# A linear-attention and token-mixing kernel: V kept in a two-tokens-per-partition layout

## The chip, the cores and the metric

One core of one Trainium2 chip. A core has TensorE (PE in the profile; its weight loads are shown apart as PEld), VectorE (DVE), ScalarE (ACT), GpSimd (POOL) and SyncE (SP, whose queue SPq issues the transfers that 16 DMA engines carry out). The metric is the device time of one execution in microseconds (us). Of several executions the median is given.

## The reference

```python
# r, k, v, w: (4 batches, 8 heads, 768 tokens, 48); u: (8, 48)
for t in range(S):
    cur = np.einsum('bhd,bhe->bhde', u[None] * kt, vt)
    y[:, :, t] = np.einsum('bhd,bhde->bhe', rt, state + cur)
    state = wt[:, :, :, None] * state + np.einsum('bhd,bhe->bhde', kt, vt)
...
x = attn_out.transpose(0, 2, 1, 3).reshape(B, S, H * D)      # (4, 768, 384)
wq, wk = x @ w_q, x @ w_k                                     # (4, 768, 64)
W_tok = scale * np.einsum('bsd,btd->bst', wq, wk)
out = np.maximum(np.einsum('bst,btd->bsd', W_tok, x), 0.0) @ w_out
```

Each head carries a 48 by 48 state that decays per key channel (w); each token adds the outer product of its key and value, and the current token counts with the extra weight u (the "bonus"). The second half mixes the tokens of a batch with a low-rank product and applies a linear layer. Since W_tok is a product of two 64-wide matrices, the kernel first forms wk^T x (64 by 384) for the batch and then multiplies by wq.

## The kernel before, in words

The recurrence is cut into chunks of 128 tokens. Two chunks make a unit of 256 tokens; 3 units make a batch, 12 units the whole. For a unit the kernel does, in the names of the steps (also the names of the tiles):

- **loads** (L489): w, k, r of 384 KB each, `load` at L237, with two consecutive tokens on a partition (64 partitions hold one chunk, so c = 0 and c = 1 are the two halves of the partitions, and j = 0, 1 is the token's parity). V comes in one of two ways, by the string `DIRECT` (L374): in 5 units like the others, in 7 units by four quarter loads (`load_v`, L229), which put one token on a partition, even tokens of a chunk on partitions 0 to 63, odd ones on 64 to 127.
- **ln, c16**: logarithm of w (lw), casts of k and r to 16 bits. **cw**: running sums of lw as matmuls with a mask. **ex**: en and ep, the exponentials of minus and plus the sum. **rT**: transposes of k and r on PE (kT, rT). **ks**: copy of kT. **qT** = rT x ks, **RT** = rT x ep, **KT** = ks x en, **ptm**: the chunk's total decay.
- **V**: in the 5 units a cast v16 (POOL, L601), four selection matmuls vp with PM (L605) that move V to one token per partition, and a copy VB out of PSUM (L615). In the 7 units only a cast VB (POOL, L596).
- **dps, dd, Vd**: the bonus weights of each token (matmuls of qT with u, L620), their copy (L630), and Vd = VB x dd on POOL (L635).
- **A, AM**: scores of a chunk, KT by RT, 16 matmuls a unit (48 rows in, 128 wide out, L643), masked by US on DVE (L653). US holds the causal mask times the key scale gv of a token.
- **kb, KD**: transposes of KT (L663) and their copy, scaled by gv (L673). **sn, SB**: the state before a chunk (a matmul of the identity with the old state, 384 columns) plus KD by VB (L684), and its decay on DVE (L698). The last chunk of a batch needs no new state.
- **y, X**: per chunk 8 matmuls of AM by VB, 48 columns each, and 4 of RT by the old state (L707); then X = y x gx + Vd on DVE (L738).
- **xt, xts, qk, qks**: transposes of X, their copy, the two projections and their copy. At the end of a batch **T** (wk^T X), then per unit **mx**, **rl** (ReLU), **fp** (by w_out), **os** and the **store**.

All matmuls go through `mm` at L191, so that the profile gives them one line and tells them apart by tile names: `PS<-VB,AM` is y's first part, `PS<-SB,RT` its second, `PS<-RT,KT` A, `PS<-CM,lw` cw, `PS<-v,PM` vp, `PS<-VB,KD` and `PS<-SB,ID` sn, `PS<-UB,qT` dps, `PS<-Z` fillers on zeros. Those that use 48 or 64 of the 128 rows of the array (cw, A, vp) come in twos on opposite halves.

The order of the work is a list made by a planner that runs while the program is built (class `Plan`). Every step has an engine, a duration, a rank and what it must follow; the planner starts the ready step of the lowest rank on each free engine, gives out the eight PSUM banks and the buffer rings, and the resulting order is the program's. Ranks are a long table of numbers (`RANK`, L312); `ENG` (L309) says for each unit which engine does a step that several could do (A for ACT, D for DVE, P for POOL). A PE step has a mode, 1 for those on half the rows; a step of the present mode has a bonus in rank (`stick`, here 10), and a change of mode is charged 90 ns. Fillers have the highest rank. Each engine then works its own list strictly in order.

Of the kernel before, what the change touches and what calls it, by code (L numbers as in the profile page):

```python
# [12 lines left out]
F32 = mybir.dt.float32  # L13
BF16 = mybir.dt.bfloat16
# [145 lines left out]
def kernel(  # L160
# [14 lines left out]
    C = 128  # L175
# [53 lines left out]
    def load_v(b, i, tl):  # L229

        for c in range(2):
            src = v[b, :, ds(i * U + c * C, C)].rearrange("h (q j) d -> j q h d", j=2)
            for j in range(2):
                nc.sync.dma_start(out=view(tl, c * DM, [[D, H], [1, D]], p0=64 * j, pn=64),  # L234
                                  in_=src[j])

# [7 lines left out]
    US = const([C, C], F32, "US")  # L244
# [4 lines left out]
    pos1 = const([C, 1], mybir.dt.int32, "pos1")  # L249
    gx = const([C, 1], F32, "gx")  # L250
    gv = const([C, 1], F32, "gv")
# [26 lines left out]
    for j in range(2):  # L278
        nc.gpsimd.iota(pos0[ds(64 * j, 64), :], pattern=[[0, 1]], base=j, channel_multiplier=2)
        nc.gpsimd.iota(pos1[ds(64 * j, 64), :], pattern=[[0, 1]], base=j + 1,  # L280
                       channel_multiplier=2)
# [14 lines left out]
    for j in range(2):  # L296
        m = view(US, 0, [[64, 2], [1, 64]], p0=j * 64, pn=64)
        nc.gpsimd.affine_select(m, m, pattern=[[1, 2], [2, 64]], compare_op=ALU.is_gt,
                                fill=0.0, base=-j, channel_multiplier=-2)

    nc.vector.tensor_scalar_mul(US, US, gv)

# [3 lines left out]
               KT=-956, ptm=-433, v16=-873, vp=-305, vb=-304, dps=-1398, vd=-510, A=-1752,  # L306
               am=2180, kb=370, kd=2179, sn=-276, sb=-57, y=-127, x=-406, xt=-2208, xts=-634,
               qk=796, qks=-45, T=-761, mx=134, rl=-215, fp=-10, os=-8, st=95, stick=-14)
    ENG = dict(k16="DPPPPPPPPPPP", r16="APPPPPPPPPPP", KT="DDPDPPPPPPPP", vb="AADDAAADAAAD",  # L309
               kd="AADAAAAAAAAA", xts="AAAAAAAADAAD", qks="AAAADAAAAAAA", rl="AAAAADAAAAAA",  # L310
               os="DAAAAAADADDA", dd="ADAAAAADAAAA", ks="DDDDDADDDADA")
# [3 lines left out]
            1000000, 1000000, 0, 17480, -4992, 450, 2230, -4819, 2230, 3580, -2227, 3580, 4930,  # L315
            315, 4930, 6280, 4423, 5750, 7042, 4130, 7599, 8203, 9637, 10305, 6520, 8450, 7220,
            9799, 9383, 8182, 7533, 10469, 8967, 9571, 10498, 9578, 10869, 10665, 11646, 12810,
            14571, 10180, 10943, 11020, 12143, 9340, 9491, 9540, 10180, 12085, 13085, 12245,
            14925, 17766, 13945, 15422, 16117, 16554, 20230, 20990, 3800, 7630, 8980, 5359, 6280,
            7630, 8120, 10330, 11680, 9560, 8980, 10330, 11886, 11510, 14832, 13007, 16113, 15138,  # L320
            12480, 15765, 15235, 18506, 17284, 16509, 15662, 15882, 15923, 17645, 17786, 18786,
            21226, 18161, 19234, 18493, 20634, 18127, 18462, 19791, 22267, 21533, 22901, 24034,
            22390, 19546, 24026, 24913, 25699, 27211, 12800, 15530, 16880, 6680, 11680, 13030,
            13880, 16880, 18230, 16380, 18230, 20230, 19932, 13171, 22133, 20817, 22948, 23977,
            14350, 23096, 11927, 25256, 24574, 22963, 25919, 25089, 26559, 27669, 28440, 25389,
            26460, 26289, 26366, 25169, 25926, 27682, 28802, 29266, 29636, 30172, 31267, 32025,
            33377, 34331, 35027, 36277, 42634, 44896, 45643, 47438, 68060, 64630, 65870, 40424,
            41218, 49147, 50444, 62246, 73160, 74400, 47931, 49305, 51271, 53304, 79580, 71920,
            73160, 18980, 20230, 21580, 21340, 22930, 24280, 22780, 24280, 25630, 25660, 26980,
            28980, 25521, 27610, 29917, 26889, 31321, 29263, 28642, 30827, 29432, 31862, 32532,  # L330
            31180, 30747, 31930, 32957, 33896, 32717, 34091, 37156, 33967, 36102, 34277, 34902,
            32317, 33017, 36557, 37244, 37511, 38427, 40144, 38057, 39136, 40754, 42035, 43054,
            43897, 19501, 21580, 22930, 24220, 25630, 26980, 27511, 28980, 30330, 32660, 34380,
            36380, 26366, 30967, 33370, 28102, 30292, 31980, 31877, 34497, 33214, 38466, 37784,
            34200, 32760, 39770, 39225, 39864, 42726, 42115, 43152, 38955, 41412, 36977, 40104,
            41298, 42554, 46608, 43554, 44151, 47308, 47764, 49883, 50497, 52931, 53981, 28540,
            30330, 31680, 29980, 31680, 33030, 31420, 33030, 34380, 37820, 40430, 42430, 34829,
            36326, 38633, 36017, 38171, 39200, 37617, 39984, 38875, 40684, 44834, 40556, 45863,
            45083, 42713, 42812, 49032, 48261, 49457, 49661, 50557, 43884, 46241, 47148, 48728,
            55306, 55676, 57228, 58272, 61887, 61643, 63369, 63826, 65200, 70240, 71791, 72987,  # L340
            74266, 78076, 76400, 77640, 68392, 70157, 75229, 75793, 77840, 79640, 80880, 78179,
            84333, 80138, 81398, 82371, 80880, 82120, 36040, 37730, 39080, 35460, 36380, 37730,
            40420, 42430, 43780, 42780, 46480, 48480, 43052, 44113, 49686, 44531, 47187, 48284,
            44758, 50831, 45385, 51474, 51799, 47560, 51346, 51566, 52629, 53486, 55438, 56273,
            59234, 57940, 58688, 53721, 54529, 50391, 52062, 55146, 57246, 60390, 61148, 62190,
            60765, 60925, 62492, 63450, 69605, 69158, 41000, 39080, 40430, 45229, 43780, 45130,
            48540, 49830, 51180, 52860, 55230, 57230, 47959, 50854, 54800, 54118, 52504, 57531,
            52116, 56126, 53151, 58894, 61199, 54277, 62137, 60557, 58699, 61966, 67582, 64953,
            61975, 62318, 63228, 60573, 62055, 63584, 64812, 66884, 65843, 66822, 67580, 68218,
            69299, 69630, 72169, 75340, 45660, 48480, 49830, 47100, 45130, 46480, 49980, 51180,  # L350
            52530, 61804, 58580, 60580, 54699, 58607, 62520, 57544, 59689, 60766, 47515, 51456,
            50715, 59283, 64030, 60716, 70782, 67826, 61497, 65731, 71002, 69344, 70247, 66715,
            67357, 63835, 64684, 70304, 71441, 71512, 72511, 73281, 76901, 77758, 78628, 80393,
            84435, 82119, 87246, 88696, 89206, 90963, 91363, 90071, 91311, 90536, 91283, 92601,
            93861, 94889, 93267, 94507, 92106, 92696, 94016, 95276, 95870, 94551, 95791, 51420,
            52530, 53880, 56567, 53880, 55230, 58347, 61930, 63280, 63845, 68570, 70570, 61097,
            63659, 66501, 65433, 69505, 69511, 66014, 70412, 67495, 71929, 72599, 68656, 73309,
# [592 lines left out]
```

## Time and profile before

| what | value |
|---|---|
| median of 3 runs | 107.58 us (107.21 to 109.12) |
| the profiled execution | 107.58 us, span of the instructions 105.9 us, granted clock 1.000 |
| units of PE work | 12, with 1503 matmul records |
| moved by DMA | 24.61 MB in 61,216 packets |
| transfers of V | 28 quarter loads of 96 KB, 5 whole ones of 384 KB |
| X on DVE (whole units) | 11 x 1014 ns |
| AM on DVE | 24 x 1219 ns |
| Vd on POOL (whole units) | 10 x 1480 ns |
| V casts on POOL | 12 x about 826 ns |

A busy share is the union of an engine's instructions over the span. Matmuls are pipelined: a record lasts from its start until its result is out, so records overlap and their mean length (183 ns for 48 columns) is far above the distance of two starts. Where the cost of a matmul matters, the starts in the timeline are read and not the lengths. A row of the timeline gathers neighbouring records of one form: start in us, length, engine, line, form, count.

### The profile page before, as it was taken

How to read it: one execution, taken by the hardware profiler on the slowest of the kernel's cores; microseconds unless marked ns; L12 is line 12 of the kernel's file. 1: busy time of each engine (PE TensorE's matmuls, PEld its weight loads, DVE VectorE, ACT ScalarE, POOL GpSimd, SP SyncE). 2: the span in 40 equal slices, each digit the busy share in tenths (PEclk: the TensorE clock that was granted, in tenths of full speed). 3: DMA queues.
4: the chain of work that ended last, by engine and by line, in shares of the span. 5: the costliest groups of instructions: out<-in, count | busy, mean ns of one | idle time of the engine just before them, and what ended most of it. 6: DMA issues, size and time to landing. Idle time of an engine off the chain costs nothing.

```text
span 105.9 us, 3705 instructions
## 1 busy us (share of the span) xinstructions
PE 97.4 (92%) x1503; PEld 69.9 (66%) x1506; DVE 86.8 (82%) x135; ACT 80.5 (76%) x121; POOL 72.4 (68%) x95
## 2 busy tenths in 40 slices
PE   5999899995988999899999799998977999999995
PEld 2346577574776698775879677895655777875651
DVE  6847789989979999979989999997686999863650
ACT  4338845986798699897999998995993798875630
POOL 6614399489796899999968998996089998000000
DMA  1999999899999989999996997899968950034374
GB/s 34 296 319 325 325 330 304 152 247 315 238 325 274 225 200 249 256 302 265 309 303 125 317 277 153 237 282 297 243 125 157 395 193 1 6 149 180 121 286 160
DMA packets 61216, 24.61 MB, mean 232 GB/s; under 512 B 58896, under 2 KB 60048, under 8 KB 61200
## 3 DMA queue, kind: packets, MB, share of 16 engines
q1 hardware_dynamic: 60640, 24.19, 84.6%
q10 hardware_dynamic: 560, 0.20, 0.7%
q8 instruction: 11, 0.18, 0.7%
q14 instruction: 5, 0.04, 0.1%
HBM read 19.66 MB, written 4.72 MB: 230 GB/s over the span
## 4 chain that ended last, share of the span: by engine, by line
PE 56%; DVE 10%; SPq 9%; POOL 9%; DMA 5%; ACT 4%; issue 3%; POOLq 0%; DVEq 0%; ACTq 0%
PE PS L191 56%; SPq L234 7%; POOL KT L582 6%; DVE AM L654 6%; DMA vg<-in_v_dram 5%; SPq L238 2%; ACT en L533 2%; POOL Vd L636 1%; DVE qT L564 1%; DVE X L741 1%; DVE SB L700 1%; ACT ep L539 1%; ACT ks L406 1%; ACT lw L502 1%; POOL r L510 1%
## 5 line engine op out<-in xcount | busy, mean ns | idle before, releaser
L654 DVE TENSOR_TENSOR AM<-PS,US 128x1024 bf16<-128x1024 f32 x24 | 28.7, 1219 | 2.7 <-PE PS L191 2.5
L636 POOL TENSOR_TENSOR Vd<-VB,dd 128x768 bf16<-128x768 bf16 (+1 forms) x14 | 18.1, 1294 | 4.0 <-ACT dd L406 2.1
L582 POOL TENSOR_TENSOR KT<-ks,en 128x1024 bf16<-128x1024 bf16 (+1 forms) x10 | 19.3, 1935 | 1.6 <-DVE ks L410 1.0
L191 PE MATMUL PS<-Z 128*128 128x512 bf16 x48 | 15.2, 443 | 1.3 <-DVE uT L256 1.2
L191 PEld LDWEIGHTS <-KT 48*128 48x128 bf16 (+1 forms) x272 | 10.5, 95 | 6.6 <-issue 3.9
L539 ACT ACTIVATE ep<-PS 128x1024 bf16<-128x1024 f32 (+1 forms) x14 | 12.8, 924 | 1.8 <-PE PS L191 1.8
L533 ACT ACTIVATE en<-PS 128x1024 bf16<-128x1024 f32 (+1 forms) x14 | 12.4, 901 | 2.2 <-PE PS L191 1.9
L741 DVE SCALAR_TENSOR_TENSOR X<-PS,gx,Vd 128x768 bf16<-128x768 f32 (+1 forms) x13 | 12.4, 953 | 2.0 <-PE PS L191 1.8
L191 PE MATMUL PS<-wo,MX 128*128 128x384 bf16 x72 | 13.3, 326 | 0.1
L502 ACT ACTIVATE lw<-wg 128x768 bf16<-128x768 f32 x12 | 10.1, 851 | 3.8 <-DMA wg<-in_w_dram 3.7
L408 ACT ACTIVATE KD<-PS,gv 128x1024 bf16<-128x1024 bf16 (+1 forms) x12 | 11.3, 945 | 1.9 <-PE PS L191 1.9
L510 POOL CAST k<-kg 128x768 bf16<-128x768 f32 x11 | 9.1, 826 | 4.3 <-PE PS L191 3.4
L700 DVE TENSOR_TENSOR SB<-PS,ptm 128x384 bf16<-128x384 f32 x20 | 11.0, 550 | 1.2 <-PE PS L191 1.2
L406 ACT COPY XT<-PS 128x768 bf16<-128x768 bf16 (+1 forms) x11 | 8.5, 773 | 2.9 <-PE PS L191 2.8
L406 ACT COPY os<-PS 128x768 f32<-128x768 f32 (+1 forms) x10 | 7.0, 703 | 3.9 <-PE PS L191 2.9
L510 POOL CAST r<-rg 128x768 bf16<-128x768 f32 x11 | 9.1, 824 | 1.1 <-DMA rg<-in_r_dram 1.1
L191 PEld LDWEIGHTS <-Z 128*128 128x128 bf16 x51 | 5.0, 109 | 6.7 <-issue 2.8
L191 PE MATMUL PS<-VB,AM 128*128 128x48 bf16 x192 | 8.4, 183 | 0.9 <-DVE AM L654 0.8
L191 PEld LDWEIGHTS <-MX 128*128 128x128 bf16 x72 | 6.5, 98 | 3.9 <-issue 0.2
L191 PE MATMUL PS<-RT,KT 48*128 48x128 bf16 x192 | 9.0, 218 | 0.0
L571 DVE TENSOR_TENSOR RT<-PS,ep 128x1024 bf16<-128x1024 bf16 (+1 forms) x14 | 8.4, 606 | 0.2 <-PE PS L191 0.2
L191 PE MATMUL PS<-ID,r 128*128 128x128 bf16 x96 | 7.2, 219 | 1.5 <-POOL r L510 0.8
(80 smaller groups left out, 205.8 us busy)
## 6 DMA issues: line engine op xcount, KB each, us to landing
wg<-in_w_dram SPq DMA_DIRECT2D x12, 384.0 KB, 5.0
kg<-in_k_dram SPq DMA_DIRECT2D x12, 384.0 KB, 5.1
rg<-in_r_dram SPq DMA_DIRECT2D x12, 384.0 KB, 5.2
out_dram<-os SPq DMA_DIRECT2D x9, 384.0 KB, 3.5
vg<-in_v_dram SPq DMA_DIRECT2D x28, 96.0 KB, 3.4
vg<-in_v_dram SPq DMA_DIRECT2D x5, 384.0 KB, 5.0
out_dram<-os SPq DMA_DIRECT2D x5, 192.0 KB, 2.0
wof<-in_moe_w_out_dram SPq DMA_DIRECT2D x1, 576.0 KB, 5.6
```

The source lines that it names most:

```text
L191: nc.tensor.matmul(o, l, rr, start=start, stop=stop, skip_group_check=True, is_transpose=trans)
L406: nc.scalar.copy(o, i)
L408: nc.scalar.activation(o, i, ACT.Copy, bias=0.0, scale=by)
L502: nc.scalar.activation(view(lw, 0, [[64, H], [512, 2], [1, D]]), view(wg, 0, [[D2, H], [D, 2], [1, D]]), ACT.Ln, bias=0.0, scale=math.exp( ...
L510: op(view(dst, 0, [[64, H], [512, 2], [1, D]]), view(src, 0, [[D2, H], [D, 2], [1, D]]))
L533: nc.scalar.activation(sb("en", [C, 1024])[:, cols(cs, 512)], t["cw"][:, cols(cs, 512)], ACT.Exp, bias=0.0, scale=-1.0)
L539: nc.scalar.activation(view(ep, cs[0] * NP * EW + 66, [[EW, NP * len(cs)], [-65, 2], [1, 64]]), t["cw"][:, cols(cs, 512)], ACT.Exp, bias=0 ...
L582: e.tensor_tensor(sb("KT", [C, 1024])[:, cols(cs, 512)], t["ks"][:, cols(cs, 512)], t["en"][:, cols(cs, 512)], ALU.mult)
L636: nc.gpsimd.tensor_tensor(sb("Vd", [C, 2 * DM])[:, cols(cs, DM)], t["VB"][:, cols(cs, DM)], view(t["dd"], cs[0] * H, [[1, len(cs) * H], [0 ...
L654: nc.vector.tensor_tensor(view(sb(f"AM{c}", [C, 1024]), 0, [[C, 8], [1, C]]), view(t[f"A{c}"], 0, [[C, 8], [1, C]]), view(US, 0, [[0, 8], ...
L700: nc.vector.tensor_tensor(view(x, 0, [[D, H], [1, D]]), view(t[f"sn{c}"], 0, [[D, H], [1, D]]), view(t["ptm"], c * 8, [[1, 8], [0, D]]), A ...
L741: nc.vector.scalar_tensor_tensor(view(X["t"], (2 * i + c0) * DM, [[DM, ncs], [1, DM]]), view(t["y"], c0 * 512, [[512, ncs], [1, DM]]), gx, ...
```

## The change

V stays in the layout of the whole load, two tokens on a partition, in all units. `load_v`, `DIRECT`, vp and VB go; every unit casts V to v16 on POOL in two instructions, one for each parity j, and multiplies by the key scale gv there, so that US becomes a mask alone and KD a plain copy. The scores are made for 64 source tokens (a chunk's even or odd ones, on the partition half of that chunk) by 128 target tokens, and each product with V is a sum over j on 64 rows. The bonus Vd = v16 x dd is in that layout too, and is brought to the output's layout by four selection matmuls with PM that add into y; X is then a scaled copy.

```diff
-    def load_v(b, i, tl):
...
-    DIRECT = "001011011011"
...
-    plan = Plan(kinds, 10, 90)
+    plan = Plan(kinds, 317, 90)
...
-    for name in ("en", "ks", "qT", "RT", "KT", "ptm", "v16", "VB", "dd", "Vd", "AM0", "AM1", "KD", "XT"):
+    kinds["v16"] = 3
+    for name in ("en", "ks", "qT", "RT", "KT", "ptm", "dd", "Vd", "AM0", "AM1", "KD", "XT"):
...
-    ENG = dict(k16="DPPPPPPPPPPP", r16="APPPPPPPPPPP", KT="DDPDPPPPPPPP", vb="AADDAAADAAAD",
-               kd="AADAAAAAAAAA", xts="AAAAAAAADAAD", qks="AAAADAAAAAAA", rl="AAAAADAAAAAA",
-               os="DAAAAAADADDA", dd="ADAAAAADAAAA", ks="DDDDDADDDADA")
+    ENG = dict(k16="APDPDAPPPPPP", r16="PPPPPPPPPPPP", KT="DDDPPPPPPDPD", kd="AADADAAADADA",
+               xts="AAADDDADADAD", qks="AAAAAADDAAAD", rl="AAAAAAAAAAAA", os="ADAAAADDAADD",
+               dd="AAADADDDDDAA", ks="DDDDADDDADDA", x="AADDAAAAAAAA")
...
+        def f_v16():
+            for j in range(2):
+                nc.gpsimd.tensor_scalar_mul(view(sb("v16", [C, 2 * DM]), j * DM, [[D, H], [1, D]]),
+                                            view(vg, j * D, [[D2, H], [1, D]]), gv[:, ds(j, 1)])
...
+        for q in range(2):
+            def f_A(q=q):
+                t[f"A{q}"] = x = wtile(f"A{q}")
+                for hl in range(2):
+                    hp = 2 * q + hl
+                    for j in range(2):
+                        for hh in range(2):
+                            for c in range(2):
+                                mm(x[ds(c * 64, 64), ds(hh * 512 + (hl * 2 + j) * C, C)],
+                                   t["KT"][ds(hh * 64, D), ds((hp * 2 + j) * C + c * 64, 64)],
+                                   t["RT"][ds(hh * 64, D), ds((hp * 2 + c) * C, C)])
...
+        kc = (0,) if last else (0, 1)
+        kn = 64 * len(kc)
+        def f_kb():
+            t["kb"] = x = stile(BF16, "kb")
+            for j in range(2):
+                for hp in range(NP):
+                    mm(x[ds(0, kn), ds((j * NP + hp) * C, C)],
+                       t["KT"][:, ds((hp * 2 + j) * C, kn)], ID16, trans=True)
...
+            for hp in range(NP):
+                for j in range(2):
+                    for c in kc:
+                        mm(t["sn"][:, ds(c * 512 + hp * D2, D2)],
+                           t["KD"][ds(c * 64, 64), ds((j * NP + hp) * C, C)],
+                           t["v16"][ds(c * 64, 64), ds(j * DM + hp * D2, D2)],
+                           start=(hp == 0 and j == 0), stop=True)
...
+        def f_y():
+            t["y"] = y = wtile("y")
+            for h in range(H):
+                hp, hh = divmod(h, 2)
+                for j in range(2):
+                    for c in range(2):
+                        mm(y[:, ds(c * 512 + h * D, D)],
+                           t[f"AM{hp // 2}"][ds(c * 64, 64),
+                                             ds(hh * 512 + (hp % 2 * 2 + j) * C, C)],
+                           t["v16"][ds(c * 64, 64), ds(j * DM + h * D, D)],
+                           start=(h == 0 and j == 0), stop=True)
+            for j in range(2):
+                for c in range(2):
+                    mm(y[:, ds(c * 512, DM)], PM[ds(c * 64, 64), ds(j * C, C)],
+                       t["Vd"][ds(c * 64, 64), ds(j * DM, DM)], start=False, stop=True)
...
+            def f_x(c0=c0, ncs=ncs, xe=xe):
+                copy(xe, view(X["t"], (2 * i + c0) * DM, [[DM, ncs], [1, DM]]),
+                     view(t["y"], c0 * 512, [[512, ncs], [1, DM]]), gx)
```

The products with the old state become steps of their own in full height (s2 in sn, y2 in y). en, ep, qT, RT and KT keep their sizes and are written in another order of columns, by head pair, then chunk or parity. A's steps now have a mode of their own (2); sn and y have mode 1. `ENG` has a new entry for X, and `RANK` is a new table throughout.

## The prediction

> **What bounds the kernel now.** I read the page first: engine shares, the forty slices, the chain.
>
> ```profile
> PE 97.4 (92%) x1503; PEld 69.9 (66%) x1506; DVE 86.8 (82%) x135; ACT 80.5 (76%) x121; POOL 72.4 (68%) x95
> DMA  1999999899999989999996997899968950034374
> PE 56%; DVE 10%; SPq 9%; POOL 9%; DMA 5%; ACT 4%; issue 3%; POOLq 0%; DVEq 0%; ACTq 0%
> ```
>
> The DMA engines are full for about three quarters of the span and PE holds 56% of the chain, so there are two candidates. The table by stage (us, then busy us of PE, weight loads, DVE, ACT, POOL, then granted clock, DMA share, GB/s) shows where each is full:
>
> ```profile
> 40.00:50.00 10.00, 9.33 (x152) 7.24 (x149) 9.26 (x13) 9.04 (x14) 10.00 (x9) 1.00 1.08 270
> 50.00:60.00 10.00, 9.22 (x193) 7.65 (x192) 9.52 (x13) 9.59 (x13) 8.31 (x10) 1.00 1.00 257
> 60.00:70.00 10.00, 10.00 (x191) 8.13 (x187) 9.91 (x14) 9.53 (x16) 9.61 (x11) 1.00 0.94 242
> 80.00:90.00 10.00, 9.65 (x178) 7.42 (x179) 8.60 (x12) 7.19 (x14) 9.60 (x12) 1.00 0.57 189
> ```
>
> Until 60 us transfers are full and PE nearly so; from 60 us PE has no idle left. But "busy" counts overlapping matmuls once, so I went on to the timeline of PE, where the step from one row's start to the next is what a run really costs (columns: start, length, form, count):
>
> ```profile
> 52.44 0.61 PE L191 MATMUL PS<-ID,k 128*128 128x128 bf16 x8
> 52.98 0.50 PE L191 MATMUL PS<-v,PM 64*128 64x384 bf16 x4
> 53.41 0.35 PE L191 MATMUL PS<-wk,XT 128*128 128x64 bf16 x6
> ...
> 54.02 0.40 PE L191 MATMUL PS<-RT,KT 48*128 48x128 bf16 x8
> 54.26 0.61 PE L191 MATMUL PS<-CM,lw 64*128 64x128 bf16 x16
> 54.80 0.62 PE L191 MATMUL PS<-ID,k 128*128 128x128 bf16 x8
> 55.26 0.33 PE L191 MATMUL PS<-VB,KD 128*128 128x96 bf16 x4
> 55.42 0.36 PE L191 MATMUL PS<-VB,AM 128*128 128x48 bf16 x8
> 55.63 0.33 PE L191 MATMUL PS<-SB,RT 128*128 128x96 bf16 x4
> 55.80 0.36 PE L191 MATMUL PS<-VB,AM 128*128 128x48 bf16 x8
> ```
>
> Full-height matmuls of 128 columns cost (55.26-54.80)/8 = 56 ns, of 96 columns 42 ns, of 48 columns (55.63-55.42)/8 = 26 ns. Those on 48 or 64 rows run in pairs, the two starts 3 to 4 ns apart in the single records: RT,KT takes 0.24 us for four pairs, 60 ns a pair. Going back to full height costs extra: CM,lw's eight pairs of 55 ns are 0.44, the step is 0.54, so a change of array shape costs 0.095 us. v,PM's step of 0.43 is two pairs of 163 ns and a change.
>
> Counts times steps, leaving out the Z fillers: 384 columns (72 wo,MX, 24 X,qk, 16 SB,ID, 10 pairs of v,PM) 122 x 163 = 19.9; qk,ts 36 x 109 = 3.9; XT,wq 3.9; k, r, KT, X transposes 344 x 56 = 19.2; 160 x 42.5 = 6.8; 288 of 48 or 2 columns x 25.2 = 7.3; wk,XT 2.1; 192 pairs x 60 = 11.5. That is 74.6 us, and 64 changes of shape in the records add 6.1: 80.7 us, 6.7 us for each of the 12 units. Gaps in the same starts beyond these costs come to 4.0 us from 10 to 33 us and 5.4 us from 33 to 97 us. PE is the nearer bound: it has 5.4 us to give after the start-up.
>
> **The change, part by part.** The sum is made against the profiled execution, 105.9 us of span and 107.58 us of time (1.7 us around it); the median of the runs is the same 107.58.
>
> PE, the part that sets the end:
>
> 1. Scores A. 16 matmuls a unit in pairs become 32 of half the width (64 of 128 output rows), which can stand four abreast. Now eight pairs, 0.48 us. Four abreast at the 128-column length: eight groups of 53 + 3 x 3.5 = 63 ns, +0.02 to +0.06 a unit; two abreast, as in the rows of today: 16 x 60 = 0.96, +0.48. No row shows four abreast; the starts 3 to 4 ns apart speak for it, so I take +0.7 us in all, ends 0 and +5.8.
>
> 2. Mix y. 16 full matmuls of 48 columns (16 x 26 = 0.41) become 32 on 64 rows. If a pair costs one step of 25 plus 3.5, 0.46 (+0.05 a unit); if each still costs 25, 0.81 (+0.40). The rows have pairs only at 128 and 384 columns, where the length hides any floor, so neither end is nearer; I take the middle, 39 ns a pair: +0.21 x 12 = +2.6, ends +0.6 and +4.8.
>
> 3. The bonus, until now added by DVE in X, becomes four PM matmuls of 384 columns in y: 12 x 2 pairs x 163 = 3.9. The same products on V (v,PM, 5 units) go: -1.6. Net +2.3.
>
> 4. Key-value products sn: pairs of 96 columns cost 46 against two of 42, so 8 units hardly change (0.03 each, 0.2), but in the four last units of a sequence only chunk 0 is needed: eight on the same 64 rows, 8 x 42 against 4 x 42: 4 x 0.17 = 0.7. Together +0.9 (0.7 to 1.2).
>
> 5. kb of those four units: eight transposes instead of four, 4 x 4 x 56 = +0.9.
>
> 6. Changes of shape. Now 41 small-array runs (12 cw, 24 A, 5 vp) make 64 changes. After: 12 cw, 24 A, 12 sn, 12 y = 60 runs, at the same ratio 94 changes, +30 x 0.095 = +2.8; the planner's bonus for staying in a shape goes from 10 to 317, which could bring this to 0. I take +1.4.
>
> Sum +0.7+2.6+2.3+0.9+0.9+1.4 = +8.8 us (lowest 4.5, highest 17.8).
>
> A rule speaks against item 2: the Trainium skill, TensorEngine Tiling (Array Packing), Performance Considerations, says under Instruction Overhead that a matmul has a fixed cost of some 60 cycles and that one should not take the tiling factor from a dimension that is already small. The trace agrees for full height (26 ns at 48 columns, 25 at 2). By the rule item 2 would be its upper end and the sum 11.0 instead of 8.8. The same page (Restrictions) says that column tiling disables fast weight load, which would push item 1 up; no row here shows a column-tiled matmul.
>
> Transfers. 28 quarter loads of V become 7 whole ones. In the packet records 14,336 packets of 192 B took 16.3 ns each, those of 384 B 22.7: 14.6 us of the 16 engines become 7,168 x 22.7/16 = 10.2, -4.5 us. On SP's queue 28 issues of 0.63 us median (17.8) become 7 of 1.1 (7.8). PE's waits for POOL's k and r casts at 78.0 and 80.2 us (0.72 and 0.76) stand behind those issues and vanish; they are among the 5.4.
>
> POOL. v16 becomes two scalar multiplications of 384. Row of 384: the wq scaling, 1170 ns (with a repeated read); casts of 192 and 768 (337, 826) put one at 500. So 1.0 to 2.3 us a unit for 0.83, +2 to +18 us; I take 1.0, as the casts are two against one. Two KT (2.13) and net two casts leave: -6.1. POOL ends near 68 (at most 85).
>
> ACT and DVE. X leaves DVE (11 x 1.01) for ACT in nine units (some 0.92: copy 0.80 plus what scaling adds to KD over a copy, 1.12 against 1.01). DVE takes KD, XT, dd, KT and k casts instead: -12 and +9, ends near 84. ACT: +8.8 and the four V evictions, three KD, four XT go: near 79. Costed at nothing: PE's own stream covers it, with 8 to 9 us of busy time in 10 already; without that cover DVE's 1.22 us AM pairs would cost first. Two more selects for US (0.29 each) lie in POOL's 5.3 idle us of the first 10; else +0.6.
>
> New waits. y on PE now waits for POOL's Vd, and behind it stands all of PE; Vd needs only dd, and comes before AM's end in the last units (83.2 to 84.7 us, AM 82.8 to 85.2), so I cost it at nothing, at most 1.5 us once in the drain. X on ACT waits for y; behind it stand the exponentials of the next unit.
>
> Now what is absorbed: a PE that is late waits for nobody, so the 5.4 us of gaps after 33 us go; those before stay. 8.8 - 5.4 = +3.4: 107.6 + 3.4 = **111.0 us**. Its own range, from small terms alone: 109 to 113.5.
>
> **Rivals.**
>
> Faster: input is the true bound. For it: the chain from 58 to 80 us runs over SP issues, V transfers and POOL. Against: PE is full from 60 to 70 us at the same time. If items 1, 2 and 6 are at their low ends (sum 4.5, less than the gaps), the stream ends 4.5 us earlier and only the last two units' extra work, 2 x 4.5/12 = 0.75, is added: 103.8. It decides when PE's addition stays under the 5.4 us.
>
> No change: PE's addition is low but the stream gains nothing, as loads wait for free buffers: 107.6 + 4.5 - 5.4, about 107.
>
> Slower: four abreast does not happen. Item 1 at its upper end: 8.8 - 0.7 + 5.8 - 5.4 = +8.5, 116.1; it decides as soon as a group of four takes 120 ns and not 63.
>
> POOL becomes the bound: v16 at 2.3. POOL is at 8.3 to 10 in 10 from 40 to 70 us; about 5.5 units lie from 30 to 70 us, each +1.5 - 0.5: +5.5, 113.
>
> **How the numbers follow.** Likeliest 0.40 (111.0), no change 0.20, input-bound 0.13, no four abreast 0.15, POOL 0.12. The range takes in the other cases but the faster one: 106 to 117. A measurement here tells 2% from nothing (2.2 us: 105.4 to 109.7). Faster 0.13; within 0.22 (no change and the low edge of the likeliest); slower 0.65.
>
> **What the profile would show.** Right: PE's share up, its gaps after 33 us gone; PS<-RT,KT groups of 32 a unit at about 16 ns each; PS<-v,AM pairs near 39 ns; no VB; q1's packets down by 7,168; last r load before 79 us. Wrong: a shorter span with PE gaps left; y pairs at 28 or 50; POOL over 80.

## The result, and the profile after

On one chip the changed kernel took 120.72 us (four runs, 120.57 to 142.27) and the kernel before 108.06 us (107.21 to 109.12): a ratio of 1.120, interval 1.108 to 1.131. Some executions run over 1.5% longer than the fastest of the same kernel, the one of 142 us among them; ratios and their intervals leave these out, and where no interval is given too few runs were left for one. The forecast was 111.0 us with a range of 106 to 117. The direction was right; the size was not, and the time lies above the range. The profiled execution after took 120.57 us with a span of 118.5 us, 12.6 us more than the span before.

The page of the changed kernel, the lines that answer to those read before: engine shares, POOL's and the DMA engines' busy tenths in 40 slices, and the chain that ended last by engine.

```profile
PE 103.8 (88%) x2010; PEld 73.8 (62%) x2014; DVE 85.4 (72%) x139; ACT 79.8 (67%) x115; POOL 86.3 (73%) x100
POOL 6633999839899949999999999999999924000000
DMA  2999999979797999999999992791303030033364
POOL 44%; PE 29%; issue 14%; DVE 9%; ACT 3%; POOLq 0%; DVEq 0%; ACTq 0%
```

PE's share fell from 92% to 88% although it has more to do; POOL went from 72.4 to 86.3 us and is 90% or more of every slice from 44 to 95 us; the chain, which lay on PE with 56%, now lies on POOL with 44%. The chain by line names the steps:

```profile
PE PS L191 29%; POOL v L589 19%; POOL Vd L609 8%; POOL KT L575 7%; POOL r L499 6%; POOL k L499 4%; POOL ptm L582 1%; DVE AM L628 1%; DVE ks L400 1%; DVE qT L554 1%; DVE k L499 1%; ACT en L522 1%; ACT ep L528 1%; DVE r L265 1%; DVE lw L259 1%
```

L589 is the new cast of V with its multiplication by gv, and the groups of the page price it (form, count, busy us and mean ns, idle before):

```profile
L589 POOL TENSOR_SCALAR v<-vg,gv 128x384 bf16<-128x384 f32 x24 | 29.5, 1240 | 0.0
```

Two of them make 2.48 us for a unit, where a cast of the whole V was about 0.83 before. The table by stage, in the columns used before:

```profile
40.00:50.00 10.00, 9.74 (x185) 7.31 (x181) 7.36 (x11) 7.03 (x11) 8.48 (x7) 0.92 1.01 267
50.00:60.00 10.00, 8.82 (x175) 6.40 (x172) 7.60 (x14) 6.96 (x9) 10.00 (x11) 1.00 1.10 295
60.00:70.00 10.00, 9.15 (x260) 6.94 (x258) 8.34 (x13) 8.61 (x10) 9.92 (x9) 1.00 1.04 278
70.00:80.00 10.00, 8.61 (x194) 6.43 (x192) 7.49 (x11) 6.73 (x9) 10.00 (x10) 1.00 0.73 228
80.00:90.00 10.00, 9.75 (x209) 7.76 (x205) 8.78 (x14) 7.99 (x10) 10.00 (x11) 1.00 0.22 84
```

The fifth engine column, POOL, is 9.9 to 10 of 10 us from 50 to 90 us; PE, which was at 10.0 from 60 to 70 us, is at 9.15 there. From 80 us the transfers are nearly over (DMA share 0.22) and POOL is still full. The chain that ended last runs mostly over POOL until 91.2 us and from there almost wholly over PE, so this stretch decides when PE can finish. POOL's timeline in it:

```profile
84.40 2.46 POOL L589 TENSOR_SCALAR v<-vg,gv 128x384 bf16<-128x384 f32 x2
86.81 0.82 POOL L499 CAST r<-rg 128x768 bf16<-128x768 f32 x1
87.59 1.48 POOL L609 TENSOR_TENSOR Vd<-v,dd 128x768 bf16<-128x768 bf16 x1
89.03 2.12 POOL L575 TENSOR_TENSOR KT<-ks,en 128x1024 bf16<-128x1024 bf16 x1
91.13 2.46 POOL L589 TENSOR_SCALAR v<-vg,gv 128x384 bf16<-128x384 f32 x2
```

One instruction follows another without a gap. KT ends at 91.15 us (89.03 + 2.12), and PE stands still for it. PE's timeline over the same stretch:

```profile
83.55 0.62 PE L191 MATMUL PS<-CM,lw 64*128 64x128 bf16 x16
84.01 0.56 PE L191 MATMUL PS<-v,AM 64*128 64x48 bf16 x32
84.42 0.49 PE L191 MATMUL PS<-Vd,PM 64*128 64x384 bf16 x4
84.83 0.42 PE L191 MATMUL PS<-RT,KT 48*64 48x128 bf16 x16
...
89.41 0.34 PE L191 MATMUL PS<-UB,qT 128*128 128x2 bf16 x8
91.21 0.62 PE L191 MATMUL PS<-ID,KT 128*128 128x128 bf16 x8 [1.46 <-POOL KT L575]
```

The bracket on the last row is 1.46 us of PE idle until KT. The waits of PE (us in all, times, longest), the first two rows before the change and the last two after it, show that such waits come more often and last longer:

```profile
PE PS L191 <- POOL KT L582: 0.8, 1, 0.8
PE PS L191 <- POOL r L510: 0.8, 1, 0.8
...
PE PS L191 <- POOL r L499: 4.6, 4, 2.0
PE PS L191 <- POOL KT L575: 2.5, 3, 1.5
```

Neither r nor KT became much dearer in itself (means of 860 ns against 824 and 2160 against 2130); they stand in POOL's queue behind L589. The gaps in PE's starts beyond what its steps cost, from 10 us on, grew from 9.7 to 16.0 us, and PE's own work by 6.4 us (worked out below); together that is the 12.6 us of the span. Some 1.3 us of the gaps are not waiting but slower steps: from 38.2 to 41.6 us PE's granted clock was about half (0.50 from 39 to 41 us).

### The profile page after: what moved, and what is told of

Read it like the earlier page. It is cut to its first block, busy times and chain, and to the rows that moved or that the text cites. A ratio compares the mean times of both kernels' runs of the same rounds, so it can differ in the third digit from the quotient of the medians.

```text
span 118.5 us, 4684 instructions
## 1 busy us (share of the span) xinstructions
PE 103.8 (88%) x2010; PEld 73.8 (62%) x2014; DVE 85.4 (72%) x139; ACT 79.8 (67%) x115; POOL 86.3 (73%) x100
## 4 chain that ended last, share of the span: by engine, by line
POOL 44%; PE 29%; issue 14%; DVE 9%; ACT 3%; POOLq 0%; DVEq 0%; ACTq 0%
PE PS L191 29%; POOL v L589 19%; POOL Vd L609 8%; POOL KT L575 7%; POOL r L499 6%; POOL k L499 4%; POOL ptm L582 1%; DVE AM L628 1%; DVE ks L400 1%; DVE qT L554 1%; DVE k L499 1%; ACT en L522 1%; ACT ep L528 1%; DVE r L265 1%; DVE lw L259 1%
## 5 line engine op out<-in xcount | busy, mean ns | idle before, releaser
L589 POOL TENSOR_SCALAR v<-vg,gv 128x384 bf16<-128x384 f32 x24 | 29.5, 1240 | 0.0
L609 POOL TENSOR_TENSOR Vd<-v,dd 128x768 bf16<-128x768 bf16 x12 | 17.7, 1475 | 2.9 <-ACT ep L528 2.3
L522 ACT ACTIVATE en<-PS 128x1024 bf16<-128x1024 f32 (+1 forms) x14 | 12.4, 900 | 7.4 <-PE PS L191 7.1
L575 POOL TENSOR_TENSOR KT<-ks,en 128x1024 bf16<-128x1024 bf16 x7 | 15.1, 2160 | 2.1 <-DVE ks L400 2.1
L191 PEld LDWEIGHTS <-KT 48*64 48x64 bf16 (+2 forms) x480 | 11.9, 105 | 6.6 <-POOL KT L575 3.1
L191 PE MATMUL PS<-Z 128*128 128x512 bf16 x47 | 13.6, 414 | 1.5 <-DVE uT L248 1.2
L528 ACT ACTIVATE ep<-PS 128x1024 bf16<-128x1024 f32 (+1 forms) x14 | 12.6, 921 | 0.0
L396 ACT COPY KD<-PS 128x1024 bf16<-128x1024 bf16 (+1 forms) x8 | 8.1, 1008 | 4.3 <-PE PS L191 4.3
L554 DVE TENSOR_TENSOR qT<-PS,ks 128x1024 bf16<-128x1024 bf16 x12 | 8.1, 685 | 3.5 <-PE PS L191 3.4
L398 ACT ACTIVATE X<-PS,gx 128x768 bf16<-128x768 f32 (+1 forms) x10 | 8.7, 869 | 1.7 <-PE PS L191 1.1
L191 PE MATMUL PS<-RT,KT 48*64 48x128 bf16 x384 | 9.5, 221 | 0.3 <-DVE SB L685 0.2
L191 PE MATMUL PS<-ID,KT 128*128 128x128 bf16 (+1 forms) x96 | 7.5, 220 | 2.5 <-POOL KT L575 2.5
L191 PE MATMUL PS<-ID,k 128*128 128x128 bf16 x96 | 7.4, 220 | 2.6 <-ACT k L499 1.3
```

The costliest lines, as they stand in the source:

```text
L191: nc.tensor.matmul(o, l, rr, start=start, stop=stop, skip_group_check=True, is_transpose=trans)
L396: nc.scalar.copy(o, i)
L522: nc.scalar.activation(part(sb("en", [C, 1024]), cs), part(t["cw"], cs), ACT.Exp, bias=0.0, scale=-1.0)
L528: nc.scalar.activation(view(ep, cs[0] * NP * EW + 66, [[EW, NP * len(cs)], [-65, 2], [1, 64]]), view(t["cw"], cs[0] * 256, [[C, 2 * len(cs ...
L554: nc.vector.tensor_tensor(view(sb("qT", [C, 1024]), 0, [[64, 2], [C, 8], [1, 64]]), view(t["rT"], 0, [[512, 2], [64, 8], [1, 64]]), view(t ...
L575: e.tensor_tensor(view(sb("KT", [C, 1024]), q0 * C, [[64, 2], [C, h8], [1, 64]]), view(t["ks"], q0 * 64, [[512, 2], [64, h8], [1, 64]]), v ...
```

## Experiments

Each batch ran on one chip together with the kernel before; "before" has a median of 108.1 to 111.2 us, depending on the chip, so times are read against that of their own batch. Where no interval is given, the median of all runs stands with its extremes. Experiments 1, 2, 4, 5, 6, 7, 8 and 13 keep the order of the kernel that they edit (8 with one filler more); in 3, 9, 10, 11, 12 and 14 the planner made another. "Planner" below is what the program's planner is told a step lasts; it moves no duration on the chip, but the order of the instructions.

**1. The scalar multiplication taken away.** Two plain casts of the same size and shape:

```diff
-                nc.gpsimd.tensor_scalar_mul(view(sb("v16", ...)...), view(vg, ...), gv[:, ds(j, 1)])
+                nc.gpsimd.tensor_copy(view(sb("v16", ...)...), view(vg, ...))
```

> The changed kernel with V cast to 16 bits by two plain copies on POOL in place of two multiplications (the factor gv is left out of V, so that part of the computation is missing). Theory POOL: the two multiplications of 1.24 us each hold POOL, whose queue feeds PE with k, r and KT; casts of 384 should be near 0.5 us each by the rows for 192 and 768 columns, so POOL gives back 24 x 0.74 = 18 us and PE becomes the bound at 107.6 + 7.3 of added PE work - 5.4 of gaps = about 109.5 us (108 to 112). Theory PE: the added matmuls and changes of shape set the time already, POOL's queue is only full because PE is late; 118 us or more. Theory wait (y on PE waits for Vd): Vd comes earlier by at most 1.5 us a unit, between the two, about 115.

Measured: 111.47 us, 1.015 of before (1.008 to 1.022). Of the 12% slowdown all but 1.5% is gone. The groups and the engine shares of this kernel:

```profile
L589 POOL CAST v<-vg 128x384 bf16<-128x384 f32 x24 | 11.9, 523 | 3.7 <-PE PS L191 2.7 <-DMA vg<-in_v_dram 1.0
PE 102.4 (93%) x2010; PEld 73.3 (66%) x2014; DVE 85.0 (77%) x139; ACT 79.9 (72%) x115; POOL 68.8 (62%) x100
```

523 ns against 1240 for the same columns; now POOL waits for PE at this line (2.7 us), where in the changed kernel nothing held it up (0.0). PE's gaps after 10 us are 8.1 us and not 16.0. The order of the instructions is that of the changed kernel on every engine, so nothing but this instruction and its price differs. The granted clock is 1.000 here and 0.986 in the changed kernel, so the 1.3 us of slower steps are part of what came back.

**2. The same product as one two-operand multiplication**, gv read with a stride of zero; the kernel then computes all that it should:

```diff
-            for j in range(2):
-                nc.gpsimd.tensor_scalar_mul(...)
+            nc.gpsimd.tensor_tensor(
+                view(sb("v16", [C, 2 * DM]), 0, [[D, H], [DM, 2], [1, D]]),
+                view(vg, 0, [[D2, H], [D, 2], [1, D]]),
+                view(gv, 0, [[0, H], [1, 2], [0, D]]), ALU.mult)
```

> The changed kernel with the same product of V and gv made by one two-operand instruction on POOL with gv read again and again, in place of two scalar multiplications. Two-operand products of 768 columns took 1.48 us (Vd), so 1.0 us a unit comes off POOL, 12 us in all. Theory POOL: POOL's busy time of 86 falls to 74, about what it was before the change (72); PE's waits for it shrink by most of the 6.6 us they grew, 111 to 114 us. Theory PE: no change beyond 1 us, 119.5 to 121. If the product of 32-bit V takes over 2.2 us, neither is tested.

Measured: 112.01 us (109.81 to 112.89) against 110.43 for before in the same batch (108.35 to 112.17). The group:

```profile
L588 POOL TENSOR_TENSOR v<-vg,gv 128x768 bf16<-128x768 f32 x12 | 18.0, 1504 | 0.6 <-DMA vg<-in_v_dram 0.6
```

So a product with a full second operand costs 1.50 us for 768 columns and the product with a scalar for each partition 2.48. POOL is busy 74.9 us here. This is the best complete version of the changed kernel; its runs overlap with those of the kernel before, so it is shown to be neither faster nor slower.

**3. The planner told the true duration**, the multiplications left as they are:

```diff
-        add("P", 960, "v16", f_v16, ...)
+        add("P", 2480, "v16", f_v16, ...)
```

> The changed kernel with the planner told 2480 ns for v16 in place of 960; the instructions are the same, only their order may change. Theory order: the loss comes from an order made for a POOL that is faster by 1.5 us a unit; 113 to 117 us. Theory POOL (capacity): POOL has the same 86 us of work ahead of the last KT, so the order helps little, 118.5 to 122.

Measured: 119.65 us, 1.085 (1.068 to 1.102). POOL is busy 86.2 us as before the edit, so the other order gives back about 3.5 points of the 12, and 8.5 remain. This order softens the load but doesn't remove it.

**4. The same load put into the kernel before.** Its V casts on POOL become two multiplications by 1.0 of 384 columns each:

```diff
-                nc.gpsimd.tensor_copy(sb("VB", [C, 2 * DM]), vg)
+                for j in range(2):
+                    nc.gpsimd.tensor_scalar_mul(sb("VB", [C, 2 * DM])[:, ds(j * DM, DM)],
+                                                vg[:, ds(j * DM, DM)], 1.0)
```

(and likewise v16 in the other five units).

> The kernel before with its V casts on POOL (0.83 us each, one a unit) replaced by two scalar multiplications by 1.0 of 384 columns each; nothing else changes. Theory POOL: 12 x (2.48 - 0.83) = +20 us on POOL (72 to 92) and about what the changed kernel lost beyond PE's share, 114 to 119 us. Theory PE: POOL has cover, since its idle time was 33 us; 107 to 110.

Measured: 114.7 us, 1.048 (1.041 to 1.056). The groups:

```profile
L598 POOL TENSOR_SCALAR VB<-vg 128x384 bf16<-128x384 f32 x14 | 16.1, 1170 | 0.0
L604 POOL TENSOR_SCALAR v<-vg 128x384 bf16<-128x384 f32 x10 | 12.1, 1223 | 0.0
```

The factor is a constant here and the input of L598 contiguous, and the price is the same within 6%: neither the scalar from memory nor the stride makes it dear, and a cast of the same size took 523 ns in experiment 1. POOL's busy time rose by 17.6 us, from 72.4 to 90.0.

**5. One multiplication of 768 instead of two of 384**, in the kernel before:

```diff
-                nc.gpsimd.tensor_copy(sb("VB", [C, 2 * DM]), vg)
+                nc.gpsimd.tensor_scalar_mul(sb("VB", [C, 2 * DM]), vg, 1.0)
```

> The kernel before with each V cast on POOL made one scalar multiplication by 1.0 of 768 columns. Two halves took 1.17 to 1.24 us each. If the price is by columns (3 ns each): 2.3 us an instruction, POOL 90 us, ratio 1.045 to 1.05, as with two halves (1.048). If half of it is a fixed cost of the instruction: about 1.8 us, POOL 84 us, ratio 1.02 to 1.04.

Measured: 113.9 us, 1.046 (1.037 to 1.054).

```profile
L597 POOL TENSOR_SCALAR VB<-vg 128x768 bf16<-128x768 f32 x7 | 14.9, 2130 | 0.4 <-issue 0.4
L601 POOL TENSOR_SCALAR v<-vg 128x768 bf16<-128x768 f32 x5 | 11.1, 2216 | 0.0
```

1170 ns at 384 and 2130 at 768 columns are 2.5 ns a column and 0.21 us fixed. The price goes by columns; joining the two would have saved a tenth. The Trainium skill, GPSIMD Engine Reference, section Engine selection, bears on this: it says that one-input work on this engine is roughly at line rate and two-input work about half as fast as VectorE. The rows come near that picture for the cast (826 ns for 768 columns, 561 on DVE) and for the two-operand KT (2130 ns for 1024 columns, 852 on DVE). For the scalar multiplication they do not: it has one tensor as input and takes longer than the product with two (2130 against 1504 ns for 768 columns).

**6. More matmuls in the kernel before**, two zero products of 384 columns for each chunk in y, 48 in all, 7.8 us of PE by the step of 163 ns:

```diff
+                for _ in range(2):
+                    mm(y[:, ds(c * 512, DM)], Z[:, ds(0, C)], t["VB"][:, ds(c * DM, DM)],
+                       start=False, stop=(old is None))
```

> The kernel before with two more full-height matmuls of 384 columns in each y (zeros times V, added into the same result), 24 x 2 x 163 ns = 7.8 us of PE, about the 7.3 us that the change added, and nothing else. Theory PE partly absorbed: PE has 5.4 us of gaps after the start-up to give, so 2 to 3 us are seen, ratio 1.02 (1.015 to 1.035). Theory PE is the bound: all of it is seen, 1.06 to 1.07. Theory transfers (PE is hidden behind the loads until 80 us and only the backlog after them counts): 1.00 to 1.01.

Measured: 112.38 us, 1.032 (1.024 to 1.041), about 3.5 us. Some 4.3 of the 7.8 us went into gaps that were there already. This tests the absorption that the prediction used (5.4 us): right in kind, a little less in size.

**7. No bonus product.** The kernel of experiment 2 without the four PM matmuls in y:

```diff
-            for j in range(2):
-                for c in range(2):
-                    mm(y[:, ds(c * 512, DM)], PM[ds(c * 64, 64), ds(j * C, C)],
-                       t["Vd"][ds(c * 64, 64), ds(j * DM, DM)], start=False, stop=True)
```

> The one-product version (V times gv in one instruction of 1.50 us on POOL), with the four selection matmuls of the bonus left out of y: the bonus is missing from the result, everything else runs, Vd too. Against the one-product version, about 1.4% above the kernel before. Theory PE (once POOL is relieved, PE's added work is what is left): 4.4 us of matmul and 12 waits less on PE, so 3 to 4 us less, a ratio of 0.98 to 0.99 to the kernel before. Theory POOL (it is still the bound with 75 us): less than 1 us, 1.01 or above.

Measured: 111.9 us (110.71 to 113.82) against 111.15 (108.44 to 111.39). A miss: PE's busy time falls from 103.3 us in experiment 2 to 99.8, the time doesn't. The steps left out come to 3.9 us, and PE's gaps grow by about as much (from 8.4 to 12.4 us). The chain shows what else holds the end:

```profile
PE 34%; SPq 21%; DMA 17%; POOL 12%; issue 7%; DVE 5%; ACT 1%; POOLq 0%; DVEq 0%
```

SP's queue and the transfers hold 38% of it. Once PE is relieved, the input stream is next in this order; less PE work in y alone did not bring the kernel under the one before.

**8. No wait for Vd.** The PM matmuls of experiment 2 read v16 in place of Vd:

```diff
-                       t["Vd"][ds(c * 64, 64), ds(j * DM, DM)], start=False, stop=True)
+                       t["v16"][ds(c * 64, 64), ds(j * DM, DM)], start=False, stop=True)
-            use=[g["v16"], g["AM0"], g["AM1"], g["Vd"]], mode=1)
+            use=[g["v16"], g["AM0"], g["AM1"]], mode=1)
```

> The one-product version with the selection matmuls kept but reading V itself in place of Vd, so that y waits for nothing on POOL beyond V (the bonus term is then not the reference's). Theory PE: same matmuls, no change, ratio 1.01 to 1.02 to the kernel before. Theory wait (PE held up by Vd): the gaps of PE ahead of the selection matmuls go, 1 to 3 us less, 0.985 to 1.005.

Measured: 112.39 us (111.23 to 112.61), same batch as experiment 7. Nothing is gained over experiment 2 (112.01 against 110.43 in its own batch): the new wait of y for Vd costs nothing that can be measured here.

**9. The planner told the price of the one product** (`960` becomes `1510` in experiment 2).

> The one-product version with the planner told 1510 ns for it in place of 960, so that its order is made for what the instruction takes; same instructions. Theory order: when the planner was told of the two multiplications the ratio went from 1.12 to 1.085, for an error of 1.5 us a unit; a third of the error should give about a third, 1 us: 1.00 to 1.01. Theory capacity: no change, 1.014.

Measured: 114.3 us (112.0 to 115.72) against 111.15. A miss: told the truth, the planner made an order that is slower and not faster (1.028 of the median before, 1.014 in experiment 2), where it had helped in experiment 3. In the new order PE's gaps after 10 us are 10.5 us against 8.4 in experiment 2, and its changes of shape 92 against 86.

**10. The scale folded elsewhere.** V is one plain cast of 768 on POOL, gv goes back into US, into KD (two half copies) and into dd:

```diff
-                nc.gpsimd.tensor_scalar_mul(view(sb("v16", ...)...), view(vg, ...), gv[:, ds(j, 1)])
-        add("P", 960, "v16", f_v16, ...)
+            nc.gpsimd.tensor_copy(view(sb("v16", [C, 2 * DM]), 0, [[D, H], [DM, 2], [1, D]]),
+                                  view(vg, 0, [[D2, H], [D, 2], [1, D]]))
+        add("P", 830, "v16", f_v16, ...)
...
+                copy(kde, sb("KD", [C, 1024])[ds(0, kn), ds(j * 512, 512)],
+                     t["kb"][ds(0, kn), ds(j * 512, 512)], gv[ds(0, kn), ds(j, 1)])
```

> The changed kernel with V cast by one plain copy of 768 on POOL (0.83 us) as before the change, and gv applied where it was before: in US, in KD (two halves with a scale, on ACT 2 x 0.70 in place of 1.01, on DVE 2 x 0.48 in place of 0.69) and in dd (a product on DVE). Planner told so. POOL falls to about 67 us, ACT rises by 8 x 0.4 = 3, DVE by 3. Theory PE: as with the plain casts (ratio 1.015) or a little better for one cast in place of two, 1.005 to 1.02: PE's added 7.3 us remain, and 5.4 of them are absorbed. If POOL alone made the change slow, 0.98 to 1.0.

Measured: 113.97 us (113.39 to 114.81) against 111.15. POOL is down to 67.1 us, less than before the change, and still it is slower than experiment 2. The order is another again (93 changes of shape, 86 in the changed kernel), so this doesn't price the fold by itself.

**11. The multiplications moved to DVE:**

```diff
-                nc.gpsimd.tensor_scalar_mul(view(sb("v16", ...)...
-        add("P", 960, "v16", f_v16, ...)
+                nc.vector.tensor_scalar_mul(view(sb("v16", ...)...
+        add("D", 740, "v16", f_v16, ...)
```

> The changed kernel with the same two multiplications of V by gv on DVE in place of POOL (planner told 740 ns for both; a 768-column cast took 0.56 us there). POOL falls from 86 to about 57 us, DVE rises from 85 to about 94. Theory POOL: the loss of the two multiplications goes whichever engine takes them over cheaply, ratio 1.01 to 1.03, as with the plain casts (1.015). Theory V late (what cost the time is that V is multiplied at all ahead of sn and y): no gain over 1.03 from here is possible, 1.06 or above. If DVE becomes the bound with 94 us: 1.04 to 1.06.

Measured: 123.94 us, 1.136 (1.125 to 1.146): worse, with POOL at 58.0 us. The tile's view of this kernel (min, median and max ns) and two rows of DVE's timeline:

```profile
L589 DVE TENSOR_SCALAR v<-vg,gv x24: 403/412/2346, 11.7 to 87.9; 128x384 bf16<-128x384 f32 x24
```

```profile
42.21 2.99 DVE L589 TENSOR_SCALAR v<-vg,gv 128x384 bf16<-128x384 f32 x2
...
49.44 0.73 DVE L589 TENSOR_SCALAR v<-vg,gv 128x384 bf16<-128x384 f32 x2
```

The same pair takes 0.73 us at 49 us and 2.99 us at 42 us. POOL's timeline beside the slow one:

```profile
41.97 2.12 POOL L575 TENSOR_TENSOR KT<-ks,en 128x1024 bf16<-128x1024 bf16 x1 [3.30 <-ACT ep L528]
44.03 0.95 POOL L499 CAST r<-rg 128x768 bf16<-128x768 f32 x1
```

KT was running when DVE began and ended at 44.09 us; the first of the pair lasts from 42.21 to 44.31 us. The second ends at 45.20 us, and the cast of r at 44.98: each time the DVE instruction ends 0.21 to 0.22 us after POOL's. The mean of the 24 is 862 ns, against 403 to 415 undisturbed, in all 20.7 us for some 9.8. The Trainium skill, SBUF — State Buffer, section Who interferes with whom, describes such a lock: the two engines share a pair of ports, a DVE scalar operation can enter a mode that needs it, and whoever has it keeps it for the whole instruction. This trace agrees in kind; whether these instructions were in that mode it does not show. How much of the 13.6% is this lock, and how much the other order, was not separated.

**12. The multiplications moved to ACT:**

```diff
+                nc.scalar.activation(view(sb("v16", ...)...), view(vg, ...), ACT.Copy, bias=0.0,
+                                     scale=gv[:, ds(j, 1)])
+        add("A", 1160, "v16", f_v16, ...)
```

> The changed kernel with the same two multiplications of V by gv on ACT (planner told 1160 ns for both). On DVE they took 0.40 us each when POOL was idle and up to 2.35 us when a POOL instruction was running, and the ratio was 1.136. Theory shared access (a DVE instruction between two SBUF tiles waits for the POOL instruction that is running; ACT does not): each takes 0.55 to 0.65 us whatever POOL does, ACT rises from 80 to about 94, POOL falls to 57, ratio 1.01 to 1.04. Theory any engine (whichever of the three gets V's product becomes the bound, since all three are full): 1.06 or above.

Measured: 119.85 us, 1.107 (1.100 to 1.114). A miss. Each takes 599 to 639 ns and is never held up; POOL falls to 58.5 us, ACT rises to 91.3, and neither is full. But the planner's order is another one, with 103 changes of shape instead of 86. The next two take order and engine apart.

**13. On ACT, in the old order** (the instructions of 12, the planner still booking 960 on POOL).

> V's two products on ACT as in the run before, but with the planner still booking 960 ns on POOL for them, so that all other instructions keep the order of the changed kernel. Theory order: 1.015 to 1.045, since the order that gave 1.015 with plain casts is back. Theory ACT: ACT has the same 91 us and now an order that does not allow for it, 1.09 or above.

Measured: 115.32 us (113.15 to 118.43) against 109.96 (107.26 to 111.37), some 5% over before. That lies between the two theories, nearer to that of the order: about half of the 10.7% of experiment 12 goes with its order, and some 3.5 points over the casts of experiment 1 (1.5%) stay with the products on ACT.

**14. Plain casts on POOL, in the order of 12** (the instructions of experiment 1, the planner booking 1160 on ACT).

> Plain casts of V on POOL (gv is left out of V, so that part of the computation is missing) in the order that the planner makes when it books 1160 ns on ACT. Theory order: 1.08 to 1.10, although POOL has 69 us and ACT 80. Theory ACT: 1.015 to 1.04, as with the plain casts in their own order.

Measured: 121.3 us (120.59 to 122.12) against 109.96. The engine shares:

```profile
PE 106.3 (88%) x2011; PEld 73.7 (61%) x2014; DVE 86.1 (72%) x139; ACT 79.7 (66%) x115; POOL 69.1 (57%) x100
```

These are the instructions of experiment 1 with the same durations (POOL 69.1 against 68.8 us, ACT 79.7 against 79.9), in another order, and it takes 121.3 us where that one took 111.5 (1.10 and 1.01 of the medians before). So an order alone is worth some 9%, here with POOL at 69.1 us and not the 86.3 of the changed kernel. This order was made for V's products on ACT and is run with casts on POOL; that of experiment 12, where the two agree, took 119.85. PE's gaps are 15.7 us against 8.1, and the changes of shape 103 against 86, which is 1.6 us. Which of the moved steps opens the gaps was not found. It means that experiments 3, 9, 10, 11, 12 and 14, in which the planner chose anew, say what a version takes and not what the edit is worth; the cause rests on 1, 2, 4 and 5, where the order stayed.

## Why the prediction was wrong, step by step

**The step that failed: POOL's v16.** "So 1.0 to 2.3 us a unit ...; I take 1.0, as the casts are two against one." It costs 2.48. The interpolation counted rows: two casts against one scalar multiplication. But the row of the same operation was that of the wq scaling, 1170 ns for 384 columns, and its repeated read, which the prediction noted beside it, does not explain the price (1170 to 1240 without it). Even the upper end of 2.3 lay below the price. Instead of 12 us for the 12 units POOL got 29.5, that is 17.5 us more than the sum assumed, and its busy time came to 86.3 us, not "near 68 (at most 85)". With it went the step that PE sets the end: the chain lies on POOL with 44% and on PE with 29%. The prediction had said that POOL over 80 would show it wrong. Taken away (1), the change costs 1.5%, and with the cheaper product (2) no more than can be told from nothing; put into the kernel before (4, 5), it costs 4.8 and 4.6% there.

**The POOL rival** named this mechanism and gave it 113 and 0.12. Its mechanism was right; its price was not. It let POOL run full only from 30 to 70 us, 5.5 units at one us. In fact POOL stayed full to 95 us, and of its 17.5 us more, some 11 show in the time (1.120 against 1.015 of experiment 1), the slower steps among them. In the kernel before, 17.6 us more on POOL cost only about 5.3 us (experiment 4), near the rival's 5.5, and another order of the changed kernel gave back 3.5 points (experiment 3): what a full POOL costs depends on the order as well, and why this order pays twice as much was not separated. When an engine becomes the bound, the sum has to be made over its whole list and not over the stretch in which it was full before.

**PE's additions** were to be +8.8. They came to +6.4. Whole runs of matmuls, from their first start to the next run's first where nothing was waited for, give 73.9 us of steps before and 77.6 after; the changes of shape are 6.1 and 8.2 us, and those out of the quarter shape cost 0.6 more. (The expectations of experiments 1, 6 and 10 say 7.3; that counts a pair as two steps where its two starts lie further apart than usual, which the starts of whole runs do not bear out.)

- Item 1, four abreast: the four starts lie 2 to 5 ns apart and a group takes 56 ns, as a pair does in the single records before (the prediction had 60). No step was added, where +0.7 was taken. Leaving this shape costs more than the 0.095 us of the others: a run of four groups takes 0.350 us to the next run and one of eight 0.573, which leaves 0.126 for the change, 0.6 us in all. The rival "four abreast does not happen" falls.
- Item 2, y: 16 pairs in 84.42 - 84.01 = 0.41 us, 25.6 ns a pair, as one full matmul of 48 columns. +2.6 was taken, +0.1 came, below the low end of +0.6. The rule that the prediction cites against splitting a small dimension (Trainium skill, TensorEngine Tiling (Array Packing), Instruction Overhead) would have given the upper end; here the measurement decides: two half-height matmuls side by side took one step together.
- Item 3, bonus: +2.2 for +2.3 (12 runs of 0.323 us without the change of shape, 3.9 us, against 1.7 on V before). Item 4: +0.7 for +0.9. Item 5: +0.9 for +0.9.
- Item 6: 86 changes of shape, where 94 stood without the planner's bonus: +2.1 for +1.4.

**Absorption** was to be 5.4 us. With the price of v16 taken out, experiment 1 gives 1.5% or 1.6 us over before, and 6.4 - 5.4 = 1.0. In the kernel before, 4.3 of 7.8 us were absorbed (6). So the PE side of the sum was right in kind and too high, +3.4 for 1.6: without the POOL step the forecast would have been 111.0 for about 109. That "slower" came true owes more to POOL than to this sum, which had 1.6 of the 12.7 us.

**A reading.** "From 60 us PE has no idle left" passes over the stage from 70 to 80 us, where PE is busy 8.31 of 10 us and waits for casts on POOL:

```profile
70.00:80.00 10.00, 8.31 (x139) 6.12 (x136) 7.92 (x12) 8.48 (x12) 6.02 (x7) 1.00 0.89 223
```

**Transfers** did what was said: 7,500 packets fewer, 23.0 ns for those of 384 B, and the last input lands at 77.9 us, not 82.4. It gave nothing: the work after the last input lasted 23.5 us before and 40.6 us after. The waits for k and r behind SP's issues went and came back as waits behind L589.

**DVE and ACT** were busy 85.4 and 79.8 us (84 and 79 forecast). X on ACT took 901 ns (0.92 forecast). **The new wait of y for Vd** was costed at nothing, and experiment 8 bears it out.

**The order** was not a step of the sum at all: the new rank table was read as part of the same stream. It was made for durations that the planner held to be true (960 ns for v16), and experiments 3 and 14 show that orders of the same work lie up to 9% apart. Whether the changed kernel has an order in which it beats the one before stays open; none of the versions tried was shown to.

## What to carry to other kernels

Price an added instruction by the row of the same operation on the same engine, even if there is only one such row and it comes from the set-up, before rows of a similar size with another operation. If that price fills an engine, sum the whole list of that engine and ask what it feeds: here late casts of r and k, in themselves hardly dearer, stopped PE. And when a planner or a rank table is given a wrong duration, test the edit in the order that is there before letting it choose anew, or two effects are measured as one.

## What was not expected of the hardware

- On POOL a multiplication by a scalar costs 2.5 ns a column (1170 ns for 384, 2130 for 768), a two-operand product 1.50 us for 768 and a cast 0.83: the operation with fewer operands is the dearer one.
- Two matmuls of 48 columns on opposite halves of the rows cost one step of 25.6 ns together; four on the quarters with 128 columns cost 56 ns.
- A DVE instruction from and to on-chip memory can last until the POOL instruction beside it has ended: 2346 ns where 404 is its own time. ACT with the same operands and the same neighbours kept to 599 to 639 ns.
- PE's granted clock fell to about half for 3.4 us, from 38.2 us on, after 1.6 us in which PE stood idle (0.91 from 30 to 40 us, 0.92 from 40 to 50 us). Idle stretches of similar length before 19 and 91.2 us were not followed by such a fall, and the cause was not found. In the profile before it was 1.00 throughout.
